# The last block of a DFT matrix and its mirror rows, fetched by one gather of 128 half rows

## The chip, the cores and the metric

The kernel runs on one core of a Trainium2 chip. The metric is the device time of one execution in microseconds; lower is better. Engines are named as in the profile: PE (matrix multiply), DVE (vector), ACT (activation), POOL (GpSimd) and SP (sync; here it only issues transfers).

## The reference

```python
x = A_x                                            # [1, 2048, 576]
n = layernorm(x)
a, b = n @ hid_re.T, n @ hid_im.T                  # 576 x 576 DFT matrices, inputs
y = seq_re @ a - seq_im @ b                        # 2048 x 2048 DFT matrices, inputs
h = x + y
z = layernorm(h)
r = z @ w_r                                        # one score a token
i = argmax(r)                                      # one token is routed
f = (silu(z[i] @ w_gate) * (z[i] @ w_up)) @ w_down # 4608 wide
out = h + z;  out[i] += f * sigmoid(r[i])
```

## The kernel before

All is in float32. The DFT matrices are inputs, and a DFT matrix is symmetric under reversal of its rows and columns. The kernel uses this to do a quarter of the products, and it *checks* on the chip that the matrices that it was given have the symmetry: for every block it loads the mirror image too, subtracts or adds the two on DVE into a bf16 strip (`Q`, two slots), and squares and sums the strip on ACT (`add_square`). If the sum is not near zero, a general path runs instead (behind a branch at the end; it does not run here).

The stages, in the order of the data:

- `x` is loaded, folded (x[d] plus and minus x[576-d]), normalized by PE with diagonal matrices, and kept as `XF`: nine folded pairs of token blocks, each with 640 columns, an even part E and an odd part O.
- The sequence matrix `ct` comes in blocks of 576 KB, straight from SP (`load_c`, line 357) and mirrored by gathers that POOL issues (`gather`, line 301, with row numbers from the table `ic`). The straight blocks of a group stay in `D0`, `D1`, `D2` (buffer D); the others and the mirrors go through a ring of seven slots of buffer R and some free D units. A slot is free when DVE has done the checks that read it (`off_s`, line 375; `off_t`, 380; `off_h`, 387).
- PE multiplies: five steps `seq` (line 565) for each of two groups, whose results DVE brings to `Z` (`keep`, 583). Then `hid` (line 610) multiplies `Z` with the hidden matrix `W`, and DVE adds the result to `X` (`residual`, 619).
- `W` is three tiles of 128 partitions, `A`, `B` and `C`, each with a real and an imaginary half of 576 columns (a "half row" is one of them). Before, A and B hold rows 0 to 127 and 128 to 255 of `wt`. C holds rows 256 to 288, real in partitions 0 to 32; the imaginary rows 256 to 287 lie in partitions 64 to 95 of the same half, since the fifth product of `hid` takes the even remainder in the upper and the odd remainder in the lower 64 partitions. The mirrors of A, B and C (rows 576 - n, by the table `iw`) are three gathers into ring slots.
- After the products: layer norm, scores, the search for the best token, then the FFN for that token. Its three weights (31.9 MB) stream through the buffers that come free (`load_ffn`, line 1181); DVE, POOL and ACT do the products and sums.

The order of everything is set by a small planner in the kernel (`Plan`): each step is added with an engine, an assumed duration and what it depends on; a simulation of the engines then fixes the order of each engine's instructions. A load has a step on SP or POOL (the issue) and one on "DMA" (its bytes over 405 GB/s). So new durations and dependencies also reorder steps that the edit does not name. Each engine and each queue works strictly in that order. `c_check(j, i)` adds a check of block j and its partner 16 - j: two straight and two mirrored blocks, two `off_s`, one `off_t`, one square. `w_first` adds SP's loads of W, `w_check` its mirrors and checks (`off_w`, lines 422 to 427), `wrap_w` (line 415) a column copy that `hid` needs.

## Time and profile before

| What | Value |
|---|---|
| median of 3 runs | 198.95 us (198.91 to 199.27) |
| profiled execution | 199.06 us, span of its instructions 197.1 us |
| busy, share of the span | DVE 84%, ACT 71%, PE 66%, POOL 57% |
| moved by DMA | 77.81 MB, mean 395 GB/s |
| of it q1 (issued by SP) | 56.56 MB, 71.1% of 16 engines' span |
| of it q0 (issued by POOL) | 21.03 MB, 26.5% |

A page of the profile cuts the span into 40 slices and gives the busy tenths of each engine and of the DMA engines; the views asked of the trace give the same for chosen windows, the instructions of one engine in order of time with what ended the idle time before them (in brackets, "<-"), and who waited for whom. "DMA share" is the mean busy share of the core's 16 DMA engines: a transfer that is busy but slow shows as a share of 1 with few GB/s, a queue with nothing to do as a share below 1. A line such as L301 is that of a helper when many operations share it. Times are from the span's start.

### The profile page before, as it was taken

The page shows a single profiled execution, that of the slowest core. Times are in us where ns is not written, and L with a number is a line of the kernel's source. Part 1 is how long each engine was busy: PE and PEld are TensorE (multiplying, and loading weights), DVE is VectorE, ACT ScalarE, POOL GpSimd, SP SyncE. Part 2 cuts the span into 40 slices and gives each one's busy share as a digit, 9 for nine tenths or more (in the row PEclk, how much of TensorE's full clock was granted, in tenths as well). Part 3 has the DMA queues.
Part 4 walks back from the last instruction along what each step waited for, and adds up shares of the span by engine and source line. Part 5 has one row for each costly group of instructions (what it writes and reads, how often), then busy time and mean ns, then how long its engine had stood idle before and what let it go on. Part 6 is the DMA issues. An engine that isn't in the chain of part 4 may idle for free. (4 is left out here: it accounts for less than half of the span.)

```text
span 197.1 us, 2789 instructions
## 1 busy us (share of the span) xinstructions
PE 130.2 (66%) x758; PEld 89.5 (45%) x758; DVE 166.4 (84%) x419; ACT 140.5 (71%) x259; POOL 111.8 (57%) x134
## 2 busy tenths in 40 slices
PE   0007889999999999999999986700241317074940
PEld 0004667755667788676866764400121103032330
DVE  4399999989899699995999999999839999987620
ACT  3298865781997879797588599989527999787600
POOL 6588888724447882398830000004556999999700
PEclk9999999999999999999999999985555555567596
DMA  5999999999999999999999999999999999999980
GB/s 183 422 412 413 409 415 406 411 394 326 401 406 396 406 379 410 409 406 415 407 408 416 422 425 419 428 421 409 430 429 417 432 423 425 423 424 421 419 354 24
DMA packets 14491, 77.81 MB, mean 395 GB/s; under 512 B 1855, under 2 KB 1859, under 8 KB 11143
## 3 DMA queue, kind: packets, MB, share of 16 engines
q1 hardware_dynamic: 10461, 56.56, 71.1%
q0 software_dynamic: 4000, 21.03, 26.5%
q8 instruction: 7, 0.11, 0.2%
q14 instruction: 13, 0.11, 0.1%
q10 hardware_dynamic: 10, 0.00, 0.0%
HBM read 72.86 MB, written 6.49 MB: 403 GB/s over the span
## 5 line engine op out<-in xcount | busy, mean ns | idle before, releaser
L368 ACT ACTIVATE Q<-Q 128x2944 bf16<-128x2944 bf16 (+5 forms) x26 | 55.4, 2132 | 15.7 <-DVE Q L380 8.2
L610 PE MATMUL py<-W,Z 128*128 128x289 f32 x180 | 45.3, 409 | 2.5 <-DVE X L619 2.5
L565 PE MATMUL ps<-D,XF 128*128 128x320 f32 (+3 forms) x216 | 44.8, 408 | 0.4 <-DMA D<-in_ct_dram 0.4
L610 PEld LDWEIGHTS py<-W,Z 128*128 128x128 f32 x180 | 33.6, 189 | 13.9 <-issue 2.2
L301 POOL DMA_INDIRECT R<-in_ct_dram,ic x21 | 29.3, 1396 | 18.0 <-DVE Q L375 14.1
L565 PEld LDWEIGHTS ps<-D,XF 128*128 128x128 f32 (+1 forms) x216 | 32.1, 172 | 12.8 <-issue 2.4
L1209 POOL TENSOR_TENSOR D<-D,Z 128x1152 f32<-128x1152 f32 x8 | 20.9, 2640 | 0.0
L667 POOL DMA_DIRECT2D out_dram<-X x1 | 0.6, 606 | 33.5 <-ACT X L661 33.5
L301 POOL DMA_INDIRECT D<-in_ct_dram,ic x11 | 14.8, 1346 | 7.6 <-DMA R<-in_ct_dram,ic 4.6
L498 ACT ACTIVATE junk<-X,XT 128x576 bf16<-128x576 f32 x16 | 12.3, 772 | 7.6 <-DVE W L459 6.4
L1214 ACT ACTIVATE junk<-D 128x576 bf16<-128x576 f32 x20 | 13.7, 683 | 3.2 <-POOL D L1209 1.6
L375 DVE TENSOR_TENSOR Q<-R,D 128x896 bf16<-128x896 f32 x11 | 11.9, 1084 | 3.9 <-DMA D<-in_ct_dram 2.4
L1236 PE MATMUL pd<-XF,H 128*1 128x144 f32 x80 | 5.3, 438 | 14.8 <-DVE H L1228 11.3
L537 PE MATMUL fo<-W,diag 128*128 128x288 f32 (+1 forms) x8 | 3.7, 640 | 16.0 <-DVE diag L528 16.0
L380 DVE TENSOR_TENSOR Q<-R,D 128x1152 bf16<-128x1152 f32 x10 | 13.4, 1348 | 0.0
L630 ACT ACTIVATE junk<-X,TD 128x576 bf16<-128x576 f32 x16 | 12.3, 766 | 1.4 <-DVE X L619 1.3
L661 ACT ACTIVATE X<-X,BB,UP 128x576 f32<-128x576 f32 x14 | 10.8, 854 | 3.1 <-DVE BB L642 3.1
L387 DVE TENSOR_TENSOR Q<-D 128x640 bf16<-128x640 f32 (+3 forms) x20 | 12.8, 694 | 0.0
L623 DVE SCALAR_TENSOR_TENSOR junk<-X,wr 128x576 bf16<-128x576 f32 x16 | 12.1, 755 | 0.3
L375 DVE TENSOR_TENSOR Q<-D 128x896 bf16<-128x896 f32 x11 | 11.8, 1082 | 0.0
L619 DVE SCALAR_TENSOR_TENSOR X<-py,X 128x576 f32<-128x576 f32 x16 | 11.6, 748 | 0.0
L375 DVE TENSOR_TENSOR Q<-R 128x896 bf16<-128x896 f32 x10 | 10.7, 1083 | 0.2 <-DMA R<-in_ct_dram,ic 0.2
(202 smaller groups left out, 257.5 us busy)
## 6 DMA issues: line engine op xcount, KB each, us to landing
D<-in_ct_dram SPq DMA_DIRECT2D x22, 576.0 KB
R<-in_ct_dram SPq DMA_DIRECT2D x10, 576.0 KB
D<-in_wu_dram SPq DMA_DIRECT2D x5, 1152.0 KB
D<-in_wd_dram SPq DMA_DIRECT2D x4, 1152.0 KB
R<-in_wg_dram SPq DMA_DIRECT2D x3, 1152.0 KB
D<-in_wg_dram SPq DMA_DIRECT2D x3, 1152.0 KB
out_dram<-X SPq DMA_DIRECT2D x2, 1440.0 KB
X<-in_x_dram SPq DMA_DIRECT2D x4, 576.0 KB
```

The source lines that it names most:

```text
L301: pool.indirect_dma_start(tile, None, view, bass.IndirectOffsetOnAxis(ap=rows, axis=0), element_offset=at)
L368: act.activation(t, t, AF.Square, accum_out=DS[0 : t.shape[0], n : n + 1])
L375: dve.tensor_tensor(o, C[j, i, True][:, 0:7, :], C[j, i, False][:, 7:0:-1, :], op=SIGN[i])
L380: dve.tensor_tensor(o, C[NK - j, i, False], C[j, i, False][:, :, ::-1], op=SIGN[i])
L387: dve.tensor_tensor(o[:, :, k::2, :], t[:, :, k::2, 0:HM], t[:, :, k::2, HM:P], op=op)
L498: act.activation(junk[:, 0:D], X[:, k, 0:D], AF.Square, bias=XT[:, n : n + 1], scale=-float(D), accum_out=VX[:, n : n + 1],)
L565: pe.matmul(cm(ZP[g, n][k % 2][p0 : p0 + m], w), XF[:, q, m0 : m0 + m], DT[g, i][:, :, k, 0:HM], start=k in (0, 1), stop=k in (6, 7),)
L610: pe.matmul(YP[GROUPS[g][c]][:, h, 0:w], Z[:, a, c * P : (c + 1) * P], w_block(a)[:, h * HD : h * HD + w], start=(a == 0), stop=(a == 4),)
L623: dve.scalar_tensor_tensor(junk2, X[:, k, 0:D], 1.0, wr, op0=OP.mult, op1=OP.mult, accum_out=TD[:, n, 0:1])
L630: act.activation(junk[:, 0:D], X[:, k, 0:D], AF.Square, bias=TD[:, n, 1:2], scale=-float(D), accum_out=VAR[:, n : n + 1],)
L1209: pool.tensor_tensor(t, t, xs.unsqueeze(1).to_broadcast([P, JW, D]), op=OP.mult)
L1214: act.activation(junk[:, 0:D], WB[w, j][:, r, :], AF.Copy, accum_out=acc[:, j + r : j + r + 1])
```

## The change

W's tiles now hold rows 1 to 128 (A) and 129 to 256 (B), and the folded columns of `XF` move with them. C becomes one tile of 128 half rows in the real half: partitions 0 to 31 real rows 257 to 288, 32 to 62 the real mirrors (319 down to 289), 63 row 0; partitions 64 to 95 the imaginary rows 257 to 288 and 96 to 127 their mirrors. One gather by a table of half rows fetches it (`iw[:, 2:3]`, made in `token_tables`). `XF` is zero in the columns that meet the mirrors, except that column 319 meets row 0. Two half rows that are only checked for being zero (rows 0 and 288, imaginary) come by a small load on SP. The gather is issued in the middle of the check (5, 0): behind the first of its two mirror gathers. It takes no slot of the ring and waits for none. The mirror gather of C goes, and the check of C gets a new form, `off_wc`, after the checks of A and B.

```diff
-E0, O0, XF_W = 0, 320, 640
+E1, E_0, O1, XF_W = 0, 319, 320, 640
+D1 = 2 * P + 1
...
+    wh = wt.rearrange("d (c e) -> (d c) e", c=2)
...
-        pool.iota(iw, pattern=[[-P, 3]], base=D, channel_multiplier=-1)
-        pool.memset(iw[0:1, 0:1], 0)
+        pool.iota(iw[:, 0:2], pattern=[[-P, 2]], base=D - 1, channel_multiplier=-1)
...
+        pool.memset(iw[:, 2:3], 0)
+        for c in range(2):
+            for p, n, row, step in ((0, 32, D1, 2), (32, 31 + c, D - D1, -2)):
+                pool.iota(iw[64 * c + p : 64 * c + p + n, 2:3], pattern=[[0, 1]], base=2 * row + c, channel_multiplier=step)
...
     def load_w(b, n):
-        name = "ABC"[n % 3]
-        if n < 3:
-            t = W[name][:, :, 0:D]
-            rows = wt[n * P : n * P + (P if n < 2 else 33), :].rearrange("p (c e) -> p c e", c=2)
-            sp.dma_start(t if n < 2 else t[0:33], rows)
-            if n == 2:
-                sp.dma_start(W[name][64:96, 0, 0:D], wt[2 * P : HD, D : 2 * D])
-            return
-        t = WM[name] = raw(b, f"w{name}m").rearrange("p a e -> p (a e)")
-        gather(t if n < 5 else t[0:33, :], wt, iw[:, n - 3 : n - 2] if n < 5 else iw[0:33, 2:3])
+        if n < 2:
+            rows = wt[n * P + 1 : (n + 1) * P + 1, :].rearrange("p (c e) -> p c e", c=2)
+            sp.dma_start(W["AB"[n]][:, :, 0:D], rows)
+        elif n == 2:
+            sp.dma_start(W["C"][0:2, 1, 0:D], wh[1 : D + 2 : D, :])
+        elif n < 5:
+            name = "AB"[n - 3]
+            t = WM[name] = raw(b, f"w{name}m").rearrange("p a e -> p (a e)")
+            gather(t, wt, iw[:, n - 3 : n - 2])
+        else:
+            gather(W["C"][:, 0, 0:D], wh, iw[:, 2:3])
...
+    def off_wc(u):
+        c, o = W["C"][:, 0, :], Q[:, u % 2, 0 : D + 289]
+        dve.memset(o[:, 0:D], 0.0)
+        for p, op in ((0, OP.subtract), (64, OP.add)):
+            dve.tensor_tensor(o[p : p + 31, 0:D], c[p + 32 : p + 63, 0:D], c[p : p + 31, 0:D], op=op)
+        dve.tensor_copy(o[32:34, 0:D], W["C"][0:2, 1, 0:D])
+        off_e(o[:, D:], c[0:64], c[64:P])
...
-    dve.memset(W["C"], 0.0)
...
         c_load(j, i, True)
+        if (j, i) == (5, 0):
+            wc_first()
...
-                "SP", then(load_w, None, n), (0.59, 0.59, 0.22)[n], LAST["SP"], users["W" + "ABC"[n]]
+                "SP", then(load_w, None, n), (0.59, 0.59, 0.005)[n], LAST["SP"], users["W" + "ABC"[n]]
...
+    def wc_first():
+        LAST["POOL"], d = load("POOL", then(load_w, None, 5), 0.295, LAST["POOL"])
+        WC.append(d)
...
+    def wc_check():
+        q, w = qs.take()
+        WS.append(add("DVE", 2.6, then(off_wc, q), WL[2], WC, w))
+        squares(q, D + 289, WS[-1])
...
-    for step in "sffsffwsss":
+    for step in "sffsffwcsss":
```

`off_e` is the last part of the old `off_w` under its own name. In the rows of the order that follow, a number after L is the line in the kernel before or in the changed one, and R, D, W, Q, X, XF are the buffers; "x2" means twice in a row.

POOL, from the loads of the first group's checks to those of the second part, before:

```order
L301 DMA D<-in_ct_dram,ic 128x896 x2
L301 DMA R<-in_ct_dram,ic 128x896 x7
L301 DMA R<-in_wt_dram,iw 128x1152
L301 DMA D<-in_wt_dram,iw 128x1152
L301 DMA D<-in_wt_dram,iw 33x1152
L301 DMA D<-in_ct_dram,ic 128x896 x2
```

and now:

```order
L308 DMA D<-in_ct_dram,ic 128x896 x2
L308 DMA R<-in_ct_dram,ic 128x896 x2
L308 DMA W<-in_wt_dram,iw 128x576
L308 DMA R<-in_ct_dram,ic 128x896 x5
L308 DMA R<-in_wt_dram,iw 128x1152
L308 DMA D<-in_wt_dram,iw 128x1152
L308 DMA D<-in_ct_dram,ic 128x896 x3
```

The gather of 33 rows behind the two other mirrors of W is gone; one of 128 half rows stands five gathers ahead of them.

DVE, around the checks of W (L422 and L423 before, L430 and L431 now), before:

```order
L375 TENSOR_TENSOR Q<-R,D 128x896
L375 TENSOR_TENSOR Q<-R 128x896
L422 TENSOR_TENSOR Q<-R,W 128x576
L423 TENSOR_TENSOR Q<-R,W 128x576
L425 TENSOR_TENSOR Q<-W 128x287
L426 TENSOR_TENSOR Q<-W 128x288
L427 CAST Q<-W 128x1
L619 SCALAR_TENSOR_TENSOR X,TD<-py_0_531,X 128x576 x2
L422 TENSOR_TENSOR Q<-D,W 128x576
L423 TENSOR_TENSOR Q<-D,W 128x576
```

and now:

```order
L382 TENSOR_TENSOR Q<-R,D 128x896
L382 TENSOR_TENSOR Q<-R 128x896
L638 SCALAR_TENSOR_TENSOR X,TD<-py_0_533,X 128x576 x2
L430 TENSOR_TENSOR Q<-R,W 128x576
L431 TENSOR_TENSOR Q<-R,W 128x576
L436 TENSOR_TENSOR Q<-W 128x287
L438 TENSOR_TENSOR Q<-W 128x288
L439 CAST Q<-W 128x1
L430 TENSOR_TENSOR Q<-D,W 128x576
L431 TENSOR_TENSOR Q<-D,W 128x576
```

The two additions to X (L619 before, L638 now) moved from behind the check of A to ahead of it; the check of C follows after two more of them.

SP, from the last blocks of `ct` to the first weights of the FFN (`wg`, `wu`, `wd`), before:

```order
L357 DMA D<-in_ct_dram 128x1152 x5
L357 DMA R<-in_ct_dram 128x1152 x3
L1181 DMA R<-in_wg_dram 128x2304
L1181 DMA XF<-in_wu_dram 128x2304
L1181 DMA XF<-in_wd_dram 128x2304
L1181 DMA D<-in_wg_dram 128x2304
L1181 DMA D<-in_wu_dram 128x2304
L1181 DMA R<-in_wd_dram 128x2304
```

and now:

```order
L364 DMA R<-in_ct_dram 128x1152
L364 DMA D<-in_ct_dram 128x1152
L364 DMA R<-in_ct_dram 128x1152 x2
L1213 DMA XF<-in_wg_dram 128x2304
L1213 DMA XF<-in_wu_dram 128x2304
L1213 DMA R<-in_wd_dram 128x2304
L1213 DMA D<-in_wg_dram 128x2304
L1213 DMA D<-in_wu_dram 128x2304
```

The first weight load goes to the space of XF, which PE reads until its last `seq` step, and no longer to R.

More of the change, by code (lines that the diff above doesn't have):

```diff
@@ L413, in wrap_w, with off_e @@
     def wrap_w(n):
[L415 removed]
+        c = 1 if n == "C" else 2
+        act.activation(W[n][:, 0:c, D : D + 1], W[n][:, 0:c, 0:1], AF.Copy)
     def off_w(n, u):
[L419 to L421 removed]
+        t, o = WM["AB"[n]], Q[:, u % 2]
+        re, im = W["AB"[n]][:, 0, :], W["AB"[n]][:, 1, :]
         dve.tensor_tensor(o[:, 0:D], t[:, 0:D], re[:, 0:D], op=OP.subtract)
         dve.tensor_tensor(o[:, D : 2 * D], t[:, D : 2 * D], im[:, 0:D], op=OP.add)
[L424 to L429 removed]
+        off_e(o[:, 2 * D : 3 * D], re, im)
+    def off_e(o, re, im):
+        h = o.shape[-1] - 289 if re.shape[0] == P else 0
+        dve.tensor_tensor(o[0 : re.shape[0], 0:287], re[:, 1:HD], re[:, D - 1 : HD : -1], op=OP.subtract)
+        o = o[:, h:] if h else o[64:P]
+        dve.tensor_tensor(o[:, 0:288], im[:, 1 : HD + 1], im[:, D - 1 : HD - 1 : -1], op=OP.add)
+        dve.tensor_copy(o[:, 288:289], im[:, 0:1])
+    def off_wc(u):
[5 more added lines that the diff above has]
+        off_e(o[:, D:], c[0:64], c[64:P])
     VX = mp.tile([P, NK], F32, name="VX")
@@ L514, in biases @@
         q = FOLDED.index(ORDER[n0])
-        d0 = XF[:, q : q + (h if n0 < 14 else 2), E0]
+        d0 = XF[:, q : q + (h if n0 < 14 else 2), E_0]
         if n0 == 14:
@@ L559, in seq @@
         ZP[g, n] = [zbank(f"ps{g}_{n}_{h}") for h in range(2)]
-        parts = [(0, E0 + 2 * P, 64, 0), (1, O0 + 2 * P, 64, 64)]
+        parts = [(0, E1 + 2 * P, 64, 0), (1, O1 + 2 * P, 64, 64)]
         if n < 4:
-            parts = [(n // 2, (E0, O0)[n // 2] + (n % 2) * P, P, 0)]
+            parts = [(n // 2, (E1, O1)[n // 2] + (n % 2) * P, P, 0)]
         for q, k in enumerate(FOLDED):
@@ L687, in then @@
         return lambda: f(*args)
-    dve.memset(XF[:, :, 289 : O0 + 1], 0.0)
-    dve.memset(XF[:, :, O0 + 288 : XF_W], 0.0)
-    dve.memset(W["C"], 0.0)
+    dve.memset(XF[:, :, E1 + 288 : E_0], 0.0)
+    dve.memset(XF[:, :, O1 + 287 : XF_W], 0.0)
     moved = [add("DMA", 1.5, None)]
@@ L862, in c_check @@
         squares(u, QW if j in PAIRS else 7 * P, n)
-    WS, WL, WRAP = [], [], []
+    WS, WL, WRAP, WC = [], [], [], []
     def w_first():
@@ L868, in w_first @@
             LAST["SP"], d = load(
-                "SP", then(load_w, None, n), (0.59, 0.59, 0.22)[n], LAST["SP"], users["W" + "ABC"[n]]
+                "SP", then(load_w, None, n), (0.59, 0.59, 0.005)[n], LAST["SP"], users["W" + "ABC"[n]]
             )
             WL.append(d)
+    def wc_first():
+        LAST["POOL"], d = load("POOL", then(load_w, None, 5), 0.295, LAST["POOL"])
+        WC.append(d)
     def w_check():
-        for n in range(3):
-            u, d = ring("POOL", load_w, (0.59, 0.59, 0.16)[n], n + 3)
+        for n in range(2):
+            u, d = ring("POOL", load_w, 0.59, n + 3)
             q, w = qs.take()
@@ L878, in w_check @@
             users[u].append(o)
-            squares(q, 3 * D, o, W_ROWS[n])
+            squares(q, 3 * D, o)
             WS.append(o)
             free.append(u)
+    def wc_check():
+        q, w = qs.take()
+        WS.append(add("DVE", 2.6, then(off_wc, q), WL[2], WC, w))
+        squares(q, D + 289, WS[-1])
     ZU = {(-1, False): users["Z"], (-1, True): users["Z"]}
@@ L961 @@
         c_half(0, c, m)
-    for j in GROUPS[0][:3]:
-        c_check(j, 0)
-    w_first()
-    for j in GROUPS[0][3:]:
+    for n, j in enumerate(GROUPS[0]):
+        if n == 3:
+            w_first()
+        if n == 4.5:
+            wc_first()
         c_check(j, 0)
@@ L976 @@
     for n in range(3):
-        WRAP.append(add("ACT", 0.25, then(wrap_w, "ABC"[n]), WL[n], SEQ[0, 2][0]))
+        WRAP.append(add("ACT", 0.25, then(wrap_w, "ABC"[n]), WL[n] if n < 2 else WC, SEQ[0, 2][0]))
     no_more("D2")
@@ L985 @@
             c_first(1, 0, (next(first),))
+        elif step == "c":
+            wc_check()
         else:
```

15 lines of the change are left out of this document (3 added, 12 removed).

## The prediction

> **What bounds the kernel now.** First the page's slices and the table of windows: which resource is never idle, and where it is slow although busy. A row has the length, then busy time of PE, PEld, DVE, ACT, POOL, then the granted TensorE clock, the DMA share and GB/s.
>
> ```profile
> DMA  5999999999999999999999999999999999999980
> 36.00:45.50 9.50, 9.50 (x47) 5.99 (x48) 8.98 (x15) 6.76 (x8) 3.47 (x3) 1.00 1.03 402
> 45.50:49.75 4.25, 4.25 (x26) 2.45 (x23) 4.25 (x6) 0.88 (x2) 2.93 (x2) 1.00 1.03 303
> 49.75:58.75 9.00, 9.00 (x35) 5.92 (x33) 8.05 (x10) 8.71 (x11) 3.80 (x4) 1.00 1.02 411
> 58.75:60.25 1.50, 1.50 (x7) 1.19 (x7) 1.50 (x5) 1.41 (x4) 1.20 (x2) 1.00 0.87 333
> 60.25:70.75 10.50, 10.50 (x45) 8.22 (x44) 8.47 (x10) 7.67 (x6) 8.37 (x8) 1.00 1.02 411
> 70.75:72.00 1.25, 1.25 (x7) 1.09 (x7) 1.25 (x6) 0.60 (x1) 0.94 (x2) 1.00 1.06 313
> 72.00:98.00 26.00, 25.34 (x109) 20.20 (x108) 23.59 (x38) 20.44 (x28) 16.85 (x11) 1.00 1.02 408
> 104.00:134.00 30.00, 20.36 (x82) 14.82 (x80) 29.59 (x69) 25.25 (x43) 0.00 (x0) 0.96 1.01 422
> 134.00:190.00 56.00, 22.48 (x270) 11.17 (x270) 45.66 (x146) 41.11 (x104) 43.77 (x31) 0.56 1.01 423
> ```
>
> The DMA engines are busy from the second slice to the 38th, and after 104 us they stream the FFN's weights at 422 to 423 GB/s without a gap. So the time is bytes over rate, plus whatever makes the stream slow or dry before 104 us. There are three such places: 45.5 to 49.75 us (303 GB/s at a share of 1.03: busy but slow), 70.75 to 72 us (313 at 1.06, the same), and 58.75 to 60.25 us (333 at 0.87: partly out of work).
>
> Next the timelines of the two issuing queues, the sizes of the odd loads, and the small read of the DMA queues in the first slow stretch (queue: packets, MB, share).
>
> ```profile
> 32.77 0.45 SPq L405 DMA_DIRECT2D W<-in_wt_dram  x1
> W<-in_wt_dram SPq DMA_DIRECT2D x1, 148.5 KB
> W<-in_wt_dram SPq DMA_DIRECT2D x1, 72.0 KB
> q0 software_dynamic: 34, 0.13, 8.9%
> 46.51 1.55 POOL L301 DMA_INDIRECT R<-in_ct_dram,ic  x1 [5.69 <-DVE Q L375]
> 57.82 1.81 POOL L301 DMA_INDIRECT R<-in_ct_dram,ic  x1 [2.73 <-DVE Q L375]
> 62.52 0.93 POOL L301 DMA_INDIRECT D<-in_wt_dram,iw  x1 [0.30 <-issue]
> 40.03 9.63 SPq L357 DMA_DIRECT2D R<-in_ct_dram  x2
> 56.57 0.33 SPq L357 DMA_DIRECT2D R<-in_ct_dram  x1
> ```
>
> W's last block (33 rows, 148.5 KB, and 32 half rows, 72 KB) ends SP's four W issues at 32.77 us, and its 33 mirror rows are the gather of 62.52. The slow stretches begin 12.7 and 8.2 us after these issues. No other load of that size goes to so few partitions, and no other stretch is slow at a full share, so I take them as the cause.
>
> Last, what the DVE waits for between 40 and 95 us.
>
> ```profile
> DVE Q L375 <- ACT Q L368: 1.5, 2, 1.0
> 66.17 1.09 DVE L375 TENSOR_TENSOR Q<-R 128x896 bf16<-128x896 f32 x1 [0.22 <-DMA R<-in_ct_dram,ic]
> 69.07 0.76 DVE L422 TENSOR_TENSOR Q<-R,W 128x576 bf16<-128x576 f32 x1 [1.80 <-DMA R<-in_wt_dram,iw]
> 71.22 0.75 DVE L619 SCALAR_TENSOR_TENSOR X<-py,X 128x576 f32<-128x576 f32 x1
> 72.57 0.75 DVE L422 TENSOR_TENSOR Q<-D,W 128x576 bf16<-128x576 f32 x1
> 93.52 1.09 DVE L375 TENSOR_TENSOR Q<-R,D 128x896 bf16<-128x896 f32 x1 [2.41 <-DMA D<-in_ct_dram]
> ```
>
> From 38 to 66 us it waits for no DMA, only 1.5 us for ACT; the loads wait for it instead (5.69 and 2.73 us on POOL). At 66.17, 69.07 and 93.52 it waits for DMA. So the two are coupled: DVE sets the pace from 42 to 60 us, DMA afterwards.
>
> **The change, part by part.**
>
> *First slow stretch.* The SP loads of 148.5 and 72 KB become two half rows (4.5 KB). The lost work is (411 - 303) x 4.25 us = 459 KB, or 1.12 us. But POOL's queue moved only 0.13 MB there, because its next gather was issued at 46.51 after 5.69 us behind DVE, and SP's second R of the 40.03 row comes at the end of its 9.63 us. DMA that is no longer slow would find those queues empty. Whatever it still gains meets the pause of 58.75 (share 0.87), where SP's load of 56.57 and POOL's gather of 57.82 were again let go by L375. Since no DVE wait before 66 us is a DMA's, an earlier landing does not make those issues earlier. Ends: 0 and 1.12 us; I take 0.1, near 0, by the 0.87.
>
> *The new gather.* It carries 128 half rows (288 KB) into all 128 partitions, on POOL just ahead of the gather of 46.51, which waited 5.69 us; at 0.93 us and 0.30 us of gap, as the row of 62.52 has, it displaces nothing. Its bytes fall into the stretch that runs out of work: 0. It needs no ring slot. Its first reader is the wrap of W, at 55 us in the row below.
>
> *Second slow stretch.* The gather of 62.52 (33 rows, 148.5 KB) goes. Here DMA is the bound (share 1.02 on both sides). Slowness: (411 - 313) x 1.25 us = 123 KB = 0.30 us. Bytes: 148.5 KB at 411 GB/s = 0.37 us. Together 0.67 us, the main term. Ends: 0.37 if something else makes the stretch slow, and 0.67.
>
> Two rules of the Trainium skill price this term otherwise; both are estimates, and neither is in the sum. "SBUF — State Buffer", Door 1 (the port swizzle): partitions 0 to 31 reach 8 of 16 DMA ports, and 0 to 63 no more, so 148.5 KB at half of 411 GB/s would lose 0.37 us instead of 0.30, and the sum would be 0.07 lower; the two rows of 303 and 313 GB/s agree in kind. "DMA: Bandwidth & Descriptors", How many engines (k): a transfer runs on the largest number of engines up to 16 that divides its rows, here 11, with three rows each. At 411/16 GB/s an engine that is 0.54 us on those 11 and nothing on the other five, and as a stream ends with its slowest engine, the sum would be 0.17 lower. The views give only the mean of the 16, so no row here decides it.
>
> ```profile
> 55.01 0.38 ACT L415 ACTIVATE W<-W 128x2 f32<-128x2 f32 x3
> 74.71 0.74 DVE L422 TENSOR_TENSOR Q<-D,W 33x576 bf16<-33x576 f32 x1
> 75.37 0.75 DVE L423 TENSOR_TENSOR Q<-D,W 33x576 bf16<-33x576 f32 x1
> 76.04 0.45 DVE L425 TENSOR_TENSOR Q<-W 33x287 bf16<-33x287 f32 x1
> 76.41 0.45 DVE L426 TENSOR_TENSOR Q<-W 33x288 bf16<-33x288 f32 x1
> 76.84 0.74 DVE L619 SCALAR_TENSOR_TENSOR X<-py,X 128x576 f32<-128x576 f32 x1
> L691 DVE MEMSET W<- x1: 1020/1020/1020, 2.2 to 2.2; 128x1154 f32 x1
> 76.95 1.64 ACT L368 ACTIVATE Q<-Q 33x1728 bf16<-33x1728 bf16 x1
> 102.56 0.93 ACT L368 ACTIVATE Q<-Q 128x896 bf16<-128x896 bf16 x1
> 14.84 0.23 POOL L484 TENSOR_TENSOR DX<-X 128x4 f32<-128x4 f32 x1 [0.52 <-DMA X<-in_x_dram,ix]
> 10.27 0.12 POOL L226 IOTA ti<- 128x2 int32 x1
> ```
>
> *DVE's check of the last block.* Before: 74.71 to 76.84 = 2.13 us. Now: a memset of 288 words (1.02 us x 288/1154 = 0.25), two subtractions of 576 at the pace of 0.67 (74.71 to 75.37), a copy of 576 (0.06 to 0.67; I take 0.67), two of 288 at 0.37, a cast at 0.06: 3.06 us, +0.9. Against it, the order puts two L619 ahead of W's first check: 71.22 to 72.57 = 1.35 us of work into the 1.80 us wait at 69.07. Net -0.45 us on DVE. That is hidden, since DVE's next long wait (93.52, 2.41 us) is for DMA; if the data came 2.41 us earlier, the cover would be gone and DVE the bound. With the two L619 displaced from the wait, the +0.9 would eat into the same 2.41 us. Behind these instructions stand ACT's squares of each check and the loads that wait for the slots of the two other mirrors; both checks start no later than the gathers land, as before.
>
> *Small parts.* The memset of 1.02 us at 2.2 us goes, before X has come: 0. ACT's square shrinks from 1.64 to about 0.93 us; ACT is busy 20.44 of the 26 us from 72 to 98: 0. POOL gets five index operations at about 0.12 us by 10.5 us, 0.6 us, against the 0.52 us it waits at 14.84: 0 to 0.1, taken as 0. W's shift by a row changes no size.
>
> *Hand-over to the FFN.*
>
> ```profile
> 99.93 0.94 POOL L301 DMA_INDIRECT D<-in_ct_dram,ic  x1 [0.30 <-issue]
> 99.84 0.33 SPq L1181 DMA_DIRECT2D R<-in_wg_dram  x1
> 102.05 0.33 SPq L1181 DMA_DIRECT2D XF<-in_wu_dram  x1
> 92.10 12.04 PE L565 MATMUL ps<-D,XF 128*128 128x256 f32 x72 [0.42 <-DMA D<-in_ct_dram]
> ```
>
> The first weight load now takes XF's space instead of R's. XF comes free when the last seq step is well on, and PE was busy nearly throughout (9.00 of 9.00 and 25.34 of 26.00 above, one wait of 0.42 at 92.10), so the load issues at about 102.05 less the gain, not at 99.84. POOL's last gather, issued until 100.87, still brings data then. Ends 0 and 2.2 us; I take 0.05, as with DMA ahead by only 0.7 us the gathers reach that far.
>
> Sum: -0.1 - 0.67 + 0.05 = -0.72 us on this execution's own 199.06 us (span 197.1), or 198.3. The runs' median is 0.11 lower: 198.95 - 0.72 = 198.2.
>
> **The rivals.** Measurement can tell about 0.2%, 0.4 us.
>
> A, the forecast, 198.2: the second stretch pays, the first does not. For it: the DVE rows.
>
> B, both pay: -1.12 - 0.67 = -1.8 us, 197.2. It needs DVE to run earlier between 42 and 60 us; for it, the new order could shorten the 1.5 us on ACT; against it, nothing of that work is taken away.
>
> C, nothing measurable, 198.9: DMA wins 0.67 us by 72 us and loses it before 104 us, through DVE's added 0.9 us if the two L619 do not fit the wait, or at the hand-over. For it: DVE is busy 23.59 of 26 us from 72 to 98.
>
> D, slower, by the hand-over alone: XF's load comes 2.2 us after the old first load, and DMA is dry for 1.6 us of it: +1.6 - 0.7 = 199.85. It decides from the point where the last gathers are moved before XF's data begin; for it, the fewer ring slots in use let gathers go earlier; against it, DMA at 98 us is the late one (2.41 us wait).
>
> **How the numbers follow.** A 0.52, B 0.14, C 0.18, D 0.16. A's own range is 197.8 to 198.7, a tenth of the cases of it within 0.4 us of before. So faster 0.61, same 0.22, slower 0.17. The range 196.9 to 199.7 takes in B with the bytes' bounds and half of D.
>
> **What would show it.** In the windows, 45.5 to 50 us without 303 GB/s, but with a share below 1 between 48 and 60 us (A) or not (B); no stretch at 313 GB/s near 71 us; the DVE's wait before W's first check under 0.5 us; the first weight load about 102 us, with a full DMA share around 103 (D: a gap of over 1 us). The prediction is wrong if either stretch stays slow with full partitions, or if the order moves a DVE wait to another check.

## The result and the profile after

The changed kernel takes 201.88 us (median of 4 runs, 201.25 to 202.62) against 199.11 us (198.91 to 199.63, 4 runs) for the kernel before on the same chip: a ratio of 1.0136, 95% interval 1.0093 to 1.0180. It is slower by 1.4%, where 0.4% faster was forecast. The profiled execution takes 201.25 us with a span of 199.5. In the table of experiments below, ratios leave out executions that lie more than 1.5% over a kernel's fastest one; several of these kernels spread further than that by themselves, so the median and range of all their executions stand beside the ratio, and where the two differ the text goes by the ratio.

The windows of the changed kernel, with the columns of the prediction's table (length, busy time of PE, PEld, DVE, ACT, POOL, granted clock, DMA share, GB/s):

```profile
36.00:45.50 9.50, 9.50 (x46) 5.99 (x46) 9.03 (x15) 6.76 (x8) 4.82 (x5) 1.00 1.04 405
45.50:49.75 4.25, 4.25 (x26) 2.45 (x23) 4.25 (x6) 0.77 (x2) 2.04 (x2) 1.00 0.99 386
49.75:58.75 9.00, 9.00 (x34) 5.98 (x32) 8.04 (x11) 8.75 (x11) 4.47 (x4) 1.00 0.98 337
58.75:60.25 1.50, 1.50 (x7) 1.17 (x7) 1.50 (x3) 1.38 (x5) 0.38 (x2) 1.00 1.03 428
60.25:70.75 10.50, 9.48 (x40) 7.17 (x39) 9.47 (x13) 7.51 (x5) 8.67 (x7) 1.00 1.03 415
70.75:72.00 1.25, 1.25 (x7) 1.09 (x7) 1.25 (x5) 1.22 (x5) 0.95 (x2) 1.00 1.00 400
72.00:98.00 26.00, 25.43 (x110) 20.26 (x108) 20.68 (x34) 17.29 (x25) 11.37 (x11) 1.00 1.02 408
98.00:104.00 6.00, 4.33 (x25) 3.34 (x26) 6.00 (x9) 4.03 (x5) 4.12 (x3) 1.00 0.96 353
104.00:134.00 30.00, 23.07 (x109) 16.70 (x104) 29.06 (x60) 24.76 (x41) 0.00 (x0) 0.97 0.99 401
134.00:190.00 56.00, 19.39 (x206) 9.53 (x206) 48.67 (x156) 43.33 (x103) 43.70 (x31) 0.53 1.00 410
```

and the one window of the kernel before that the prediction did not show:

```profile
98.00:104.00 6.00, 6.00 (x46) 4.01 (x44) 6.00 (x11) 5.03 (x9) 2.27 (x3) 1.00 1.02 408
```

Both slow stretches are gone (386 for 303 GB/s, 400 for 313). The rate then drops in four later places: 337 for 411 GB/s from 49.75 to 58.75 us, 353 for 408 from 98 to 104, 401 for 422 from 104 to 134, and 410 for 423 from 134 on. From 72 to 98 us the DMA is as full as before, but DVE is busy 20.68 us for 23.59: it stands 2.9 us longer.

DVE's timeline shows where (start, length, engine and line, tiles, and in brackets the wait ahead of it):

```profile
69.45 0.75 DVE L430 TENSOR_TENSOR Q<-R,W 128x576 bf16<-128x576 f32 x1
...
75.17 0.30 DVE L444 MEMSET Q<- 128x288 uint32 x1
75.50 1.53 DVE L446 TENSOR_TENSOR Q<-W 31x576 bf16<-31x576 f32 x2
77.06 0.45 DVE L447 CAST Q<-W 2x576 bf16<-2x576 f32 x1
77.52 0.45 DVE L436 TENSOR_TENSOR Q<-W 64x287 bf16<-64x287 f32 x1
...
78.55 1.09 DVE L382 TENSOR_TENSOR Q<-D 128x896 bf16<-128x896 f32 x1
...
96.62 1.09 DVE L382 TENSOR_TENSOR Q<-D,R 128x896 bf16<-128x896 f32 x1 [5.15 <-DMA R<-in_ct_dram]
```

The wait before W's first check is gone (69.45 has none). The wait at 93.52 us, 2.41 us for a block in D, has become one of 5.15 us. It is the same check, that of j = 10, i = 0, and the same straight block of `ct`; only its buffer is another (R for D).

Behind that check stand Z's copies (L602), for which PE waits next, in PE's timeline:

```profile
99.70 7.33 PE L584 MATMUL ps<-D,XF 128*128 128x256 f32 x50 [1.67 <-DVE Z L602]
```

SP's queue in the changed kernel, its stands at that line from 70 to 84 us (17/28/6574 ns are the shortest, the middle and the longest), and then SP's queue before:

```profile
63.85 18.89 SPq L364 DMA_DIRECT2D D<-in_ct_dram  x5
82.79 0.42 SPq L364 DMA_DIRECT2D R<-in_ct_dram  x1
...
104.93 0.33 SPq L1213 DMA_DIRECT2D XF<-in_wg_dram  x1
...
150.17 0.39 SPq L1092 DMA_DIRECT2D out_dram<-X  x2
```

```profile
L364 SPq EVENT_SEMAPHORE  x5: 17/28/6574, 64.2 to 83.7; - x5
```

```profile
74.02 7.68 SPq L357 DMA_DIRECT2D D<-in_ct_dram  x5
...
146.08 0.40 SPq L1060 DMA_DIRECT2D out_dram<-X  x2
```

SP stands up to 6.6 us among the five loads into D, and the awaited block goes out at 82.79 us (81.31 before, the last of the five). The FFN's first load comes at 104.93 us (99.84 before). The stores of X under a condition are issued when the FFN's token is known, so the last row is a mark on the way to the end: **the token comes 4.1 us later**, 150.17 for 146.08.

### The profile page after: what moved, and what is told of

Same layout as the page of the kernel before. It is cut to its first block, busy times and chain, and to the rows that moved or that the text cites. A ratio compares the mean times of both kernels' runs of the same rounds, so it can differ in the third digit from the quotient of the medians.

```text
span 199.5 us, 2784 instructions
## 1 busy us (share of the span) xinstructions
PE 129.5 (65%) x758; PEld 89.7 (45%) x758; DVE 166.8 (84%) x420; ACT 140.0 (70%) x259; POOL 109.1 (55%) x138
## 4 chain that ended last, share of the span: by engine, by line
DVE 26%; POOL 21%; issue 20%; DMA 15%; PE 12%; ACT 2%; SPq 0%; POOLq 0%; DVEq 0%
PE py L629 7%; DMA R<-in_ct_dram 7%; DVE junk L642 5%; POOL R L308 5%; POOL D L1241 5%; DMA X<-in_x_dram,ix 4%; DMA D<-in_wt_dram,iw 4%; PE pd L1268 3%; DVE Q L382 3%; DVE Q L387 2%; DVE X L638 2%; PE spin L1278 2%; ACT Q L375 1%; DVE D L478 1%; POOL W L1241 1%
## 5 line engine op out<-in xcount | busy, mean ns | idle before, releaser
L375 ACT ACTIVATE Q<-Q 128x2944 bf16<-128x2944 bf16 (+5 forms) x26 | 54.7, 2104 | 18.8 <-DVE Q L387 11.0
L308 POOL DMA_INDIRECT R<-in_ct_dram,ic x22 | 25.6, 1164 | 20.6 <-DVE Q L382 16.0
L382 DVE TENSOR_TENSOR Q<-R,D 128x896 bf16<-128x896 f32 x16 | 17.3, 1084 | 1.4 <-ACT Q L375 1.4
L1241 POOL TENSOR_TENSOR D<-D,Z 128x1152 f32<-128x1152 f32 x7 | 18.2, 2622 | 0.0
L1246 ACT ACTIVATE junk<-D 128x576 bf16<-128x576 f32 x18 | 12.3, 684 | 2.8 <-POOL D L1241 2.3
L387 DVE TENSOR_TENSOR Q<-R,D 128x1152 bf16<-128x1152 f32 x9 | 12.2, 1350 | 1.0 <-DMA R<-in_ct_dram 1.0
L638 DVE SCALAR_TENSOR_TENSOR X<-py,X 128x576 f32<-128x576 f32 x16 | 11.5, 750 | 0.6 <-PE py L629 0.6
L1268 PE MATMUL pd<-D,H 128*1 128x144 f32 x160 | 7.9, 356 | 5.9 <-DVE H L1260 4.9
L262 PE MATMUL pmt<-ident,gt 128*128 128x128 f32 x4 | 1.2, 453 | 15.4 <-DVE gt L267 15.4
L556 PEld LDWEIGHTS fo<-W,diag 128*128 128x128 f32 x8 | 2.5, 324 | 17.0 <-DVE diag L547 16.1
```

What stands on the lines that cost most here:

```text
L308: pool.indirect_dma_start(tile, None, view, bass.IndirectOffsetOnAxis(ap=rows, axis=0), element_offset=at)
L375: act.activation(t, t, AF.Square, accum_out=DS[0 : t.shape[0], n : n + 1])
L382: dve.tensor_tensor(o, C[j, i, True][:, 0:7, :], C[j, i, False][:, 7:0:-1, :], op=SIGN[i])
L387: dve.tensor_tensor(o, C[NK - j, i, False], C[j, i, False][:, :, ::-1], op=SIGN[i])
L638: dve.scalar_tensor_tensor(t, y, 1.0, t, op0=OP.mult, op1=OP.add, accum_out=TD[:, n, 1:2])
L1241: pool.tensor_tensor(t, t, xs.unsqueeze(1).to_broadcast([P, JW, D]), op=OP.mult)
```

## The experiments

The list of free load buffers (`free`) is a ring: a load takes its first buffer, a check puts its buffers back at the end. In the kernel before, the 33 mirror rows of W-C took one of these buffers, D's second. The new gather takes none, so every later load of the checks uses the buffer that the load after it had before. I call that the buffers' turn. A new turn also makes the planner order some checks anew, and the word takes that in.

Theory 1: the turn costs the time (1a by the FFN's first load, which now goes to XF; 1b by DVE's wait, which delays the token; 1c by SP's stand ahead of the block that DVE waits for). Theory 2: the new data path itself costs it. Theories D and L, which split 1c, stand in e13's expectation. All kernels, us:

| kernel | median (range, executions) | before, beside it | ratio, 95% interval |
|---|---|---|---|
| e5 changed, again | 202.23 (199.31 to 203.66, 6) | 199.64 (29) | 1.0141, 1.0098 to 1.0185 |
| e1 turn +1 | 200.18 (198.21 to 202.40, 12) | 199.54 (35) | 1.0010, 0.9982 to 1.0039 |
| e4 turn +2 | 198.88 (197.56 to 201.33, 12) | 199.54 (35) | 0.9950, 0.9923 to 0.9976 |
| e14 turn +3 | 198.38 (197.88 to 201.80, 6) | 199.84 (23) | 0.9921, 0.9899 to 0.9943 |
| e15 turn +4 | 197.91 (197.31 to 198.82, 6) | 199.84 (23) | 0.9901, 0.9878 to 0.9924 |
| e13 turn +1, later loads alone | 199.02 (198.03 to 200.88, 12) | 199.84 (23) | 0.9958, 0.9924 to 0.9992 |
| e6 turn +1, first FFN load in XF | 198.98 (197.93 to 200.48, 12) | 199.64 (29) | 0.9974, 0.9952 to 0.9997 |
| e3 first FFN load in R | 200.84 (198.47 to 202.63, 12) | 199.54 (35) | 1.0002, 0.9963 to 1.0042 |
| e7 one check later on DVE | 200.92 (199.03 to 202.68, 12) | 199.64 (29) | 1.0058, 1.0031 to 1.0084 |
| e8 e1 and 2.7 us of DVE | 202.46 (199.58 to 204.62, 12) | 199.64 (29) | 1.0089, 1.0056 to 1.0122 |
| e18 e15 and 2.7 us of DVE | 199.71 (198.30 to 201.25, 12) | 199.54 (23) | 1.0011, 0.9983 to 1.0038 |
| e9 two blocks first | 207.29 (202.22 to 208.95, 6) | 199.42 (11) | 1.0189, 1.0145 to 1.0233 |
| e10 e6, two blocks first | 205.26 (204.09 to 206.63, 6) | 199.42 (11) | 1.0294, 1.0257 to 1.0330 |
| e11 before, two blocks first | 204.49 (202.34 to 207.91, 6) | 199.42 (11) | 1.0157, 1.0141 to 1.0173 |
| e12 e6 and loads to few partitions | 199.29 (198.27 to 200.50, 6) | 199.42 (11) | 0.9999, 0.9968 to 1.0029 |
| e16 before, turn +1 | 200.61 (199.36 to 206.99, 14) | 199.84 (23) | 1.0019, 0.9997 to 1.0040 |
| e2 before, turn +2 | 203.26 (198.95 to 205.76, 12) | 199.54 (35) | 1.0022, 0.9988 to 1.0057 |
| e17 before, turn +3 | 201.85 (199.70 to 203.38, 12) | 199.54 (23) | 1.0081, 1.0050 to 1.0112 |

**The turn or the data path: e5, e1, e2.** e5 is the changed kernel. e1 puts the turn back, e2 spoils that of the kernel before:

```diff
     def wc_check():              # e1; e4, e14, e15 with 2, 3, 4
+        free.extend(free[:1])
+        del free[:1]
         q, w = qs.take()
...
             free.append(u)       # e2, end of w_check before; e16, e17 with 1, 3
+        free.extend(free[:2])
+        del free[:2]
```

> The changed kernel itself, unaltered, so that its time stands beside the runs of the other kernels on the same chip. Both theories: 201 to 203 as a median, 1.0% to 1.8% over the kernel before; its lowest run not under 200.5 if DVE's wait of 5.15 us comes in every execution, and down to 199 if it depends on how the transfers happen to fall.

> The changed kernel, with one line more: before W-C's check takes its Q buffer, the list of free load buffers is moved on by one, as the old gather of W-C's mirrors did when it took a buffer and gave it back. Nothing else of the data path changes, and every load, gather and check of the second half then uses the buffer and stands at the place that it had before the change; the first FFN weight load goes to R again. Theory 1 (the buffers' turn: without W-C's third gather every later block moves to the next buffer, so R's buffer 4 is held by one of the last gathers and the FFN's first load waits for XF): the first FFN load is back at about 99 to 101 us (104.93 in the changed kernel), DVE's wait for R near 92 us falls from 5.15 us to under 3, and the time is 198.0 to 199.1, at or a little under the kernel before. Theory 2 (the new data path costs the time: W-C's check takes DVE 3.4 us for 2.1, and the gather stands in POOL's queue): nothing of this changes and the time stays at 201 to 202.5.

> The kernel before, with its data path untouched, and the list of free load buffers moved on by two after W-C's check; by this the first FFN weight load has no early buffer in R or D either and waits for XF. Theory 1 (the buffers' turn): the first FFN load comes at 104 to 105 us for 99.84, the transfers fall under 350 GB/s between 100 and 107 us, and the time is 200.8 to 202.5, as in the changed kernel. Theory 2 (the new data path costs it): 199.1 as before, within 0.3.

The changed kernel again took 202.23 us, 1.0141 of the kernel before. Its profiled execution was the shortest of the six, 199.31 us, and DVE did not wait for the block of j = 10 in it, though SP issued the block 3.1 us later than in the profile above. Rows of POOL, DVE and SP:

```profile
61.23 6.63 POOL L308 DMA_INDIRECT D<-in_wt_dram,iw  x1 [0.30 <-issue]
```

```profile
74.61 0.81 DVE L430 TENSOR_TENSOR Q<-D,W 128x576 bf16<-128x576 f32 x1 [4.06 <-issue]
...
94.47 1.08 DVE L382 TENSOR_TENSOR Q<-D,R 128x896 bf16<-128x896 f32 x1
```

```profile
85.87 0.42 SPq L364 DMA_DIRECT2D R<-in_ct_dram  x1
...
148.16 0.39 SPq L1092 DMA_DIRECT2D out_dram<-X  x2
```

The gather of W's second mirror held POOL 6.63 us (1.09 in the profile above), and DVE stood 4.06 us ahead of that mirror's check instead (the view names no releaser). So the long wait for one block does not come in every execution of the changed kernel, as the second case of e5's expectation has it: the turn alone does not fix it.

e1, with the same data path as e5, took 200.18 us, a ratio of 1.0010 for 1.0141, though its median lies above the 198.0 to 199.1 that I expected. In e1's profiled execution (198.21 us) SP, DVE and the hand-over stand as theory 1 said, in timeline rows of SP and of DVE:

```profile
73.52 9.70 SPq L364 DMA_DIRECT2D D<-in_ct_dram  x5
...
100.09 0.33 SPq L1215 DMA_DIRECT2D R<-in_wg_dram  x1
...
146.45 0.39 SPq L1094 DMA_DIRECT2D out_dram<-X  x2
```

```profile
93.77 1.09 DVE L382 TENSOR_TENSOR Q<-R,D 128x896 bf16<-128x896 f32 x1 [1.81 <-DMA D<-in_ct_dram]
```

The first load is back at 100.09 us, the wait at 1.81. e2's executions fall into two groups: five of up to 200.9 us, which alone enter its ratio of 1.0022 (0.9988 to 1.0057), and seven of 202.7 to 205.8, of which none was profiled (the profiled one took 199.00). So e2 does not show clear of noise that its turn slows the kernel before, and what the second group waits for is not known. For the new data path the turn's effect is shown, by e5 and e1 and by e4, e14 and e15 below; theory 2 falls as the whole cause.

**Which part of the turn: e6, e3, e7.** e6 is e1 with the first FFN load sent to XF again. e3 leaves the turn and gives the first load a pair in R. e7 changes only DVE's order:

```diff
         at = {b: over(ns) for b, ns in spots.items()}
+        at[9] = at[11] + 0.01        # e6 (with e1's lines); e3: at[9] = 0.0
...
-    for n in range(0, N_RAW - 1, 2):  # e3
+    for n in range(1, N_RAW - 1, 2):
...
-            n.append(add("DVE", 1.08, then(off_s, m, i, u, 1), d2, d3, w))   # e7
+            n.append(add("DVE", 1.08, then(off_s, m, i, u, 1), d2, d3, w, push=-3.0 if (m, i) == (10, 1) else 0.0))
```

> e1's kernel (list of free buffers moved on by one, checks in the order of before), with one line more: the FFN's first two loads are told to wait for XF, and R's early pair gets the third, as in the changed kernel. So the first load is late and DVE's order is the good one. Theory 1a (the first FFN load in XF costs it: the transfers have nothing to do from 101 us until XF is free): first load at 102 to 103 us, 1.5 to 2 us of transfer time lost, and the time 199.8 to 200.8 in its better runs, about 1.5 us over e1's 198.2. Theory 1b (DVE's idle time before the token is known costs it; transfers lost at the hand-over are made good later while the loads wait for buffers anyway): no more than 0.7 us over e1's better runs, 198.2 to 199.

> The changed kernel with the turn of its buffers as it is, but R's buffers are given to the FFN as the pairs 1-2, 3-4, 5-6 in place of 0-1, 2-3, 4-5, and the FFN's first load is told to take the pair 5-6, which no gather after about 86 us uses. DVE's checks of the second half change places with this, since the planner sees another work behind them. Theory 1, with the first load as the whole cause: the first FFN load at 99 to 102 us and the time 198.3 to 199.5. Theory 1, with DVE's wait of 5.15 us for a block in R as the cause (it holds the Z copies back that PE, and so XF, wait for): XF comes free as late as in the changed kernel, at about 105 us; one load alone fills 2.9 us of the gap, and the time is 199.5 to 201. Theory 2 (the new data path): 201 to 202.5.

> The changed kernel, its buffers' turn, loads and gathers all as they are on SP and POOL, with one number more for the planner: the check of j = 10, i = 1 (the one whose block in R DVE waits 5.15 us for) loses its place, so that DVE does residuals, other checks and Z copies first; the first FFN load still goes to XF. Theory 1a (first FFN load in XF): the time stays within 1 us of the changed kernel, 200.5 to 202, unless XF comes free more than 2 us earlier. Theory 1b (DVE's idle time): DVE waits under 2.5 us in sum between 72 and 98 us (5.32 in the changed kernel, 2.41 before), the first store under SP's condition, which marks when the token is known, comes at 146 to 147.5 us (150.17 in the changed kernel, 146.08 before), and the time is 198.2 to 199.8. Theory 2 (the new data path): 201 to 202.5.

e6 took 198.98 us, a little less than the kernel before, with its first load in XF:

```profile
101.54 0.33 SPq L1215 DMA_DIRECT2D XF<-in_wg_dram  x1
...
145.76 0.39 SPq L1094 DMA_DIRECT2D out_dram<-X  x2
```

So 1a falls: where DVE is in time, XF comes free at 101.5 us, and that load costs nothing. e3 (1.0002) and e7 (1.0058) won back part or all of e5's loss (1.0141), but e3's first load still came only at 103.34 us, and its checks on DVE changed places too. In e7, DVE's wait was still 3.65 us: its check that I had moved, j = 10, i = 1, was not the one that waits (the rows above belong to j = 10, i = 0). Their medians, 200.84 and 200.92 us, lie between the theories, and they decide nothing more.

**Does the token set the end: e8, e18.** Each doubles one check on DVE after the hand-over:

```diff
-        for k, op in enumerate((OP.subtract, OP.add)):
+        for k, op in enumerate((OP.subtract, OP.add) * (2 if (g, c) == (1, 0) else 1)):
+            k %= 2
```

> e1's kernel with one check of the last group (two differences of 128 x 576 elements in each half, four instructions, some 2.7 us of DVE in all) done twice, about 117 us into the program, well after the FFN's first loads are out. Nothing at the hand-over changes. Theory 1b (DVE paces the way to the token, and the time follows the token once the slack is used up): token 2.7 us later than in e1, at about 149.1 us, and the time 200 to 200.6 in its better runs, 1.7 to 2.4 over e1's. Theory 1a (the hand-over's lost transfers): 198.2 to 199, as e1. This run also gives the slack: 2.7 us less what the time rises.

> e15's kernel with the one check of the last group done twice, as in e8: 2.7 us more of DVE between 115 and 122 us, after the hand-over. e15's DVE waits 0.4 us between 72 and 98 us and its token is known at 144.1 us. Theory 1b (DVE's way to the token paces the end once its slack is used up; the profiled executions so far stay at 197.7 to 198.2 us with the token at 144.1 to 146.9 us, and lie above 200 with it at 148.4 or later): token at 146.8, and the time no more than 0.7 us over e15's, 198 to 198.6, since the slack takes most of the 2.7 us. Rival (no slack: DVE bounds the kernel throughout): 200 to 200.7.

For 2.7 us of work on DVE, e8 rose by 1.6 us over e1 by the ratios (1.0089 for 1.0010; 1.7 to 2.4 were expected) and e18 by 2.2 us over e15 (1.0011 for 0.9901; at most 0.7 were expected, and the rival without slack had 2.1 to 2.8); by the medians it is 2.3 and 1.8. So DVE's way to the token sets the end, with 0.5 to 1.1 us of slack, less than I had reckoned for e15. e8's profiled execution, the longest of its twelve (204.62 us), also waited 7.67 us for a block in D, so its token (153.85) tells nothing of the 2.7 us. The profiled executions say it more sharply. First the row of the token in e15, e14 and e18 (e6's and e1's stand above), one fence for each:

```profile
144.08 0.39 SPq L1094 DMA_DIRECT2D out_dram<-X  x2
```

```profile
146.88 0.39 SPq L1094 DMA_DIRECT2D out_dram<-X  x2
```

```profile
147.55 0.39 SPq L1095 DMA_DIRECT2D out_dram<-X  x2
```

Those executions took 197.70 (e15), 197.93 (e6, 145.76), 198.21 (e1, 146.45), 197.99 (e14) and 199.19 us (e18). Up to a token at 146.9 the time is 197.7 to 198.2, whatever the token; I take the transfers for that bound, which no experiment tests. From there on it is the token plus 51 us: 51.6 in e18, 51.1 in the changed kernel (201.25 less 150.17), 51.2 in e5 (199.31 less 148.16), and 50.8 to 51.7 in e3, e4, e7, e12 and e13. The two profiles of the changed kernel show it best, since they are of one kernel: from 36 to 134 us DVE stood 8.72 us in one and 6.68 in the other, the tokens lie 2.01 us apart and the times 1.94. 1b holds there.

It does not cover every kernel. In e9, e10, e11, e16 and e17 the end comes 52.0 to 54.3 us after a token of 148.8 us or later, so there something else is late too: e9 and e10 lose transfers at the hand-over (below), and e11, e16 and e17 have the old data path. That path seems to have a higher floor: the kernel before took 199.06 us with the token at 146.08, e2's profiled execution 199.00 with it at 144.73:

```profile
144.73 0.40 SPq L1062 DMA_DIRECT2D out_dram<-X  x2
```

**The block moved ahead: e9, e10, e11.** The block that DVE waits for is issued behind four blocks that are needed later. Here the straight blocks of j = 10 and j = 9 go first:

```diff
-    c_first(1, 1)
     for i in range(2):
-        for j in GROUPS[1]:
+        for n, j in enumerate(GROUPS[1]):
+            if (i, n) == (0, 2):
+                c_first(1, 1)
             c_check(j, i)
```

> The changed kernel with one thing moved in SP's queue: the straight blocks of j = 10 and j = 9 (i = 0, into R and D), which stand behind the four straight blocks of the last group's sine half (into D's first buffers), stand ahead of them. In the changed kernel SP stands 6.6 us at the second of those four (73.4 to 79.7 us), until a check gives its buffer in D back, and then issues five loads in a burst up to 82.8 us; the block of j = 10, the last but one of the burst, is what DVE waits 5.15 us for. Buffers' turn, gathers and the first FFN load in XF stay as in the changed kernel. Theory 1c (the turn gives the second of the four a buffer whose check comes late, SP's queue stands, and DVE waits for the block behind it): DVE idle from 72 to 98 us falls from 5.32 to under 2.5 us, the token is known at 146 to 147.5 us, the time 198.5 to 199.8 as a median (202.23 for the changed kernel on this chip). Rival (the block lands late because POOL's gathers take their share of the transfers, wherever it stands): the wait stays over 3 us or moves to another block, and the time stays over 201.

> e6's kernel (the changed kernel, list of free buffers moved on by one, FFN's first load in XF) with the same two straight blocks ahead of the four. Theory 1c: DVE idle from 72 to 98 us under 1.5 us (1.91 in e6), and since the transfers bound it then, the time 197.3 to 198.8, at or a little under e6's 198.98, with a narrower spread than e6's 197.93 to 200.48. Rival: 199 to 200.5, since the four blocks come later now and PE's Z, and with it XF, late.

> The kernel before with the same two straight blocks ahead of the four. In it DVE waits 2.41 us for the block of j = 10. Theory 1c together with a bound by the transfers (422 GB/s from 98 us to the end): the wait goes, and the time falls by no more than 0.6 us, to 198.9 to 199.6 on a chip where before takes 199.6. If DVE bounds the kernel before as well: 197.3 to 198.3.

None of the expected gains came. e10 is 3.2% slower than e6 (1.0294 for 0.9974) and e11 1.6% slower than the kernel before; e9 (1.0189) cannot be told from e5 (1.0141) by the ratios, while its median is 5 us higher. In e10's profile (205.50 us) DVE waits for no block between 84 and 105 us, but PE now waits for the four blocks, as e10's rival had it, at a far lower price. PE's timeline, a window, and SP's next load:

```profile
98.83 13.37 PE L584 MATMUL ps<-D,XF 128*128 128x256 f32 x70 [5.45 <-DMA D<-in_ct_dram]
```

```profile
104.00:110.00 6.00, 6.00 (x37) 4.70 (x37) 5.05 (x10) 5.47 (x9) 0.00 (x0) 1.00 0.07 27
```

```profile
110.32 0.33 SPq L1216 DMA_DIRECT2D XF<-in_wg_dram  x1
```

The late PE holds XF, so the FFN's first load waits until 110.32 us and the transfers stand for nearly 6 us (27 GB/s). e9's profile shows the same. I had called the four blocks "needed later" without looking at what waits for them next. So these runs cannot price 1c. e5's profile speaks against it as the whole cause: the block went out 3.1 us later there, and DVE did not wait for it.

**What in the turn: e13, e4, e14, e15.** e13 turns the list only after `no_more("D0")`, so that SP still stands at D's second buffer; e4, e14 and e15 free two, three and four of D's buffers for the four blocks.

> The changed kernel with the list of free buffers moved on by one only after the checks of the first group, when D's first five buffers have left the list. So D's second buffer is still taken by the mirrors of a later check, as in the changed kernel, SP stands at the second of the four straight blocks until about 79 us, and only the later loads change their buffers. Theory D (SP's stand at D's second buffer is the cause): 201.3 to 202.8 as a median, DVE idle from 72 to 98 us over 3.5 us. Theory L (the turn of the later loads is the cause): 199 to 200.5, as e1.

> The changed kernel with the list of free buffers moved on by two in place of one: the loads then use other buffers than in either kernel, but a pair of D's buffers is free early for the FFN's first load (the plan has it earlier than any other turn). Theory 1 (what counts is that some buffer is free for the FFN before XF): the first FFN load before 101 us, and 198.0 to 199.3. A rival within it (what counts is the exact order of before): 200 to 202. Theory 2 (the new data path): 201 to 202.5.

> The changed kernel with the list of free buffers moved on by three at W-C's check. Of the four straight blocks none waits for a check's buffer any more: the plan has them out at 73 us (the changed kernel: one; moved on by one: two; by two: three). The later loads take the buffers that they take in e2, which had two kinds of execution, 199 to 200.9 and 202.7 to 205.8, and the FFN's first load goes to XF. Theory D: 198 to 199.3 as a median, at or under e4's 198.88. Theory L: as e2, 201 to 204 as a median, some executions under 200.

> The changed kernel with the list moved on by four: the four straight blocks out early as in e14, another later turn, and a pair of D's buffers early for the FFN's first load. Theory D: 198 to 199.3, as e14. Theory L: its own time, which nothing tells beforehand: 198 to 204, and not the same as e14's within 1 us.

e13 took 199.02 us (0.9958) with SP's stand in place, against theory D; its profiled execution (198.56 us) still had DVE stand 4.0 us from 72 to 98 us, as D had it, nearly all of it for the block:

```profile
95.00 1.09 DVE L382 TENSOR_TENSOR Q<-R,D 128x896 bf16<-128x896 f32 x1 [3.86 <-DMA D<-in_ct_dram]
```

e4, e14 and e15 fall in steps to 197.91 us, as theory D has it, and e14 is fast with the later turn of e2 (a median of 203.26 us), against theory L. So neither is the whole cause: e13 moved only the later loads' buffers and gained, and D's steps fit the early ones. What exactly makes the block land late in the changed kernel's own turn stays open. e15 beats both kernels, 0.9901 (0.9878 to 0.9924). Its windows:

```profile
45.50:49.75 4.25, 4.25 (x24) 2.49 (x21) 4.25 (x6) 0.96 (x2) 3.01 (x2) 1.00 1.02 405
49.75:58.75 9.00, 9.00 (x34) 5.92 (x33) 8.05 (x11) 8.66 (x12) 3.73 (x4) 1.00 0.98 366
...
70.75:72.00 1.25, 1.25 (x8) 1.09 (x7) 1.25 (x4) 1.25 (x3) 0.73 (x1) 1.00 0.98 394
72.00:98.00 26.00, 25.75 (x112) 20.87 (x111) 25.62 (x41) 19.98 (x29) 14.87 (x12) 1.00 1.02 409
```

From 72 to 98 us DVE stands 0.38 us.

**The data path at one turn: e16, e17.**

> The kernel before, its data path untouched, with the list of free buffers moved on by one after W-C's check, which gives all later loads the buffers that they have in e4 (the changed kernel moved on by two, 198.88 as a median and 0.995 of the kernel before). The difference to e4 is the two data paths' at one turn. If the new data path saves what the prediction's main term said (0.3 us of the second slow stretch and 0.37 us of bytes, some 0.7 us): 199.3 to 199.9. If it saves nothing and e4's gain is the turn's: 198.6 to 199.1. Theory L, with a turn that suits one data path alone: over 200.5.

> The kernel before, its data path untouched, with the list of free buffers moved on by three after W-C's check, which gives all later loads the buffers that they have in e15 (the changed kernel moved on by four, 0.990 of the kernel before). If e15's gain is the new data path's (a slow stretch fewer and 0.37 us of bytes, 0.7 to 1.1 us): 199 to 200, about 1 to 1.5 over e15's 197.91. If it is the turn's: 197.8 to 198.5. If the old data path suits no turn but its own (as in e2 and e16): over 200.5.

At the turns of e4, e14 and e15 the ratios of the old data path (e16 1.0019, e2 1.0022, e17 1.0081) lie 0.7%, 1.0% and 1.8% above the new one's (0.9950, 0.9921, 0.9901); by the medians it is 0.9% to 2.5%. At the old path's own turn the two are equal: e1's ratio is 1.0010 (0.9982 to 1.0039). e17's median is in the third case of its expectation (over 200.5 us); e16 lies between its cases. The old path gains by none of the three turns and clearly loses by e17's, where the new one gains by all three. So the turn and the data path do not add up. The old path at the turn of the changed kernel itself was not run.

**The cause of the slow stretches: e12.**

```diff
             sp.dma_start(W["C"][0:2, 1, 0:D], wh[1 : D + 2 : D, :])
+            for p, n in ((2, 32), (34, 32), (66, 32)):
+                sp.dma_start(W["C"][p : p + n, 1, 0:D], wt[2 * P : 2 * P + n, 0:D])
```

> e6's kernel with three loads more on SP, behind W's: 32 half rows each into 32 partitions of W-C that nothing reads, 96 packets of 2304 B in all, as many as the old loads of W-C's 33 and 32 rows had, 0.22 MB. It asks for the cause of the slow stretch at 45.5 to 49.75 us of the kernel before (303 GB/s at a full share). Prediction's step 1 (loads into few partitions slow everything that moves beside them): a stretch of 2 to 4 us between 40 and 50 us under 330 GB/s at a share over 1, with packets of D's loads and gathers taking longer; the time no more than 0.3 us over e6's, since DVE paces that part. Rival (the stretch was slow for another reason, the place of the loads or the gathers' rows): over 380 GB/s up to 48 us, as in e6.

```profile
45.50:49.75 4.25, 4.25 (x27) 2.40 (x23) 4.25 (x6) 0.64 (x2) 1.90 (x2) 1.00 1.02 309
49.75:58.75 9.00, 9.00 (x35) 6.03 (x33) 8.04 (x11) 8.75 (x11) 4.48 (x4) 1.00 1.03 412
```

The slow stretch is back (309 GB/s at a share of 1.02, 303 at 1.03 in the kernel before; 380 at 0.96 in e6), the dry one after it is gone (412 GB/s; 373 in e6), and the median is 0.3 us over e6's. (Its profiled execution, 200.50 us, had DVE wait 5.52 us for the block of j = 10, where e6's, at the same turn, waited 1.74.) So 0.22 MB into 32 partitions at a time are enough to make a stretch slow, as the prediction took it. The second stretch goes with the 33-row gather in the profiles of the old path too: in e11 that gather's packets run from 73.7 to 75.2 us, and the rate from 73.75 to 75.25 us is 321 GB/s, where 70.75 to 72 us has 415. The Trainium skill says of copies between cores, in "DMA: Bandwidth & Descriptors", Back-pressure in remote DMA, that a saturated destination port clogs the way for other engines, and that stalled writes stall an engine's other queues; these rows show a like slowing for loads from HBM (309 and 303 GB/s), but not that a port is what saturates. The rule that the prediction quoted from that page for 33 rows (11 engines of 16) gives 16 engines for 32 rows, and the stretch is as slow: by that rule, the number of engines is not its cause.

## Why the prediction was wrong, point by point

- **First slow stretch, taken at 0.1 us: right.** The changed kernel moves 386 for 303 GB/s in it, 353 KB more, and 666 KB less in the 9 us after it (337 for 411). e15 nets 28 KB: (405 - 303) x 4.25 less (411 - 366) x 9, from e15's windows above. The gain is given back where the prediction said, since DVE sets the pace there.
- **Second slow stretch and bytes, 0.67 us: right in the rates, not always won in time.** 400 for 313 GB/s over 1.25 us is 0.26 us for the 0.30; the 0.37 us of bytes were not measured by themselves. In the profiles with an early token the new path ends at 197.7 to 198.2 us and the old one at 199.0 to 199.1, 0.8 to 1.4 us apart, where the sum said 0.72. But at the turn of the kernel before (e1) the ratio is 1.0010 (0.9982 to 1.0039), and the 0.4% of the forecast lies outside this interval. e6, at the same turn with the first FFN loads in XF, has 0.9974 (0.9952 to 0.9997). So at the old turn the gain in time lies between nothing and the forecast, and e1's best executions alone (198.2 us) show all of it.
- **DVE's check of W-C, +0.9 us: low.** It takes 3.38 us (75.17 to 78.55), 1.25 over the old one: the memset comes to 0.33 with its gap (0.25 in the sum), the two subtractions to 1.56 (1.34), the last three instructions to 1.03 (0.80), and the copy of two rows gives back 0.2. That W's first check would no longer wait was right.
- **"Hidden, since DVE's next long wait is for DMA": this step failed.** I took 2.41 us of waiting at 93.52 us as cover of a fixed size. The wait ends when one block lands, and that moves: it was 5.15 us in the changed kernel's first profile and nothing in its second (e5), where 4.06 us stood at W's second mirror instead. In the first, over 36 to 134 us DVE stood 8.72 us for 6.32, the sums of its idle time in the windows; with 1.25 us more work that is 3.65 of the 4.1 us by which the token is late; in e5 it is 0.36 and 1.25 of 2.08. How much slack the old path's token had was never worked out, since the prediction followed the transfers to the end and not the token. If the 51 us held for it, it would be 2 us (199.06 less 51 is 148.1, against 146.08); with the 52.0 us of e16 it would be 1, and neither is shown.
- **"It needs no ring slot": the step that began it.** I priced this at nothing. With the slot's turn given back and nothing else changed, the ratio falls from 1.0141 (e5) to 1.0010 (e1). In the order that stands ahead of the prediction, one buffer's name after another differs from there on, and I read that for the first FFN load alone.
- **Hand-over, 0.05 us: low here, but not the cause.** The first load came 5.1 us later, not 2.2, because PE waited for DVE's late Z copies. From 98 to 104 us the transfers lost (408 - 353) x 6 = 330 KB, 0.8 us. e6 shows that the place of the load costs nothing by itself.
- **Rival D** had the sign, but named the hand-over alone at 1.6 us as its mechanism, and e6 rules that out. "If the order moves a DVE wait to another check" was close: in the first profile the wait stayed at its check and doubled, in e5 it did move to another.
- **Rival C** had DVE's added work eat the gain. At the old turn (e1, 1.0010) the time is as C had it; a loss of 1.4% was in no rival.
